# One set of products a batch in place of three, and a new order for the whole program: attention numerators of two batches on 32x32 tiles

## The chip, the cores and the metric

One core of a Trainium2 chip runs the kernel. The metric is the device time of one execution in microseconds (us). Before the change the median of three runs was 218.81 us (217.84 to 220.41).

The engines are named as in the profile: PE (TensorE, matmul), DVE (VectorE), ACT (ScalarE), POOL (GpSimd), and the DMA queues that SP, ACT and POOL feed.

## The reference: what is computed

A polynomial-sketch attention, then a token-mixing block on its output. Cut to what matters:

```python
def phi(x):                                  # r = 8, so 64 features
    a, b = S1 @ x, S2 @ x                    # per batch, head, token
    return outer(a, b)                       # (..., 64)
q_p, k_p = phi(q), phi(k)
kv  = einsum('bhsf,bhsd->bhfd', k_p, v)
num = einsum('bhsf,bhfd->bhsd', q_p, kv)     # what the change rearranges, for batches 2 and 3
den = einsum('bhsf,bhf->bhs', q_p, sum_s k_p) + 1e-6
x = num / den                                # 4 batches, 4 heads of 32, 1088 tokens -> (4, 1088, 128)
theta = x @ w_theta
zr, zi = x * cos(theta), x * sin(theta)
y = w_tok_r @ zr + w_tok_i @ zi              # two 1088 x 1088 mixes per batch
u = x + y
out = u + relu(u @ w_ch)
```

The weights arrive as 64-bit floats; the kernel turns them into 32-bit floats on the chip.

## The kernel before

**Stages.** For each batch: sums over the keys (`sums`, `rest`), key features and their products with v (`kT`, `kf`, `kv`), a small chain that fixes scales (`chain`), query slices (`qT`, `q0`), query features by exact slices (`levels`), the denominator (`den`), the numerator (`num`), theta with its sine and cosine, which gives z (`theta`), then the mix over tokens (`mix`) and the output product (`out`). Tokens are in 9 chunks of 128; three chunks make a group g (0, 1, 2), 384 columns. The rows of `w_tok` come in 17 blocks: each is loaded (L642), converted by two ACT instructions (L643, L645) and two DVE instructions (L647, L649), and only then used by `mix`. Batches 0 and 1 are mixed directly (`mix_row`); 2 and 3 together by seven half-size products (`winograd`: `m1` to `m7`), whose operands POOL and DVE add up (`asum`, `zsub`).

**Order.** Nothing is decided at run time. Every step is an `op` with an engine; the tuple `ORDER` lists all steps in the order in which they are issued, and each engine works its part of that list in order. `STARTS` holds a planned start for each, from which `run` (L248) picks buffers, and from which `issue` (L267) fills planned waits of PE between two marked steps with idle products: `spin` (L427), 384 columns of zeros that nobody reads, five for each planned us (`FILL`). 39 shorter ones (L431) run at the very start.

**Buffers.** Classes of equal buffers (L344): `zs` has 5 of 2176 words (z, the raw weight rows, copies for turning), `g3` 5 of 768, and so on.

**The numerator of batches 2 and 3** (`QUADS`, L1106 to L1123). For each of the three groups, DVE makes the outer products `qp` and turns them in 32x32 blocks into `qt` (class `g3`); `quads` (L1112) then runs 32 products for the group: 2 feature halves f x 4 row blocks j x 4 heads h, each with a 32x32 stationary block and 3 x 32 = 96 moving columns, on the tile of the array at row block j and column block h. f = 0 and f = 1 add up in one PSUM bank for each j. ACT copies the four banks to `xT` (L1121). In the trace an f32 product leaves two matmul records, so that a group has 64.

**The end.** `finish` (L1282) makes the output product, adds it (L1294), turns the result on DVE (L1303) and stores it. For batch 3's first half it starts the stores right there (L1304 to L1307: one on ACT's queue, one on SP's, two on POOL's). The last 160 columns of that half go through `finish_turned` (L1329), where PE turns the columns itself and the two stores write whole rows.

Of the kernel before, what the change touches and what calls it, by code (L numbers as in the profile page):

```python
# [22 lines left out]
P = 128  # L23
# [55 lines left out]
)  # L79
STARTS = (  # L80
# [58 lines left out]
)  # L139
WARM = 0  # L140
FILL = 5.0
LOAD_LEAD = 60.0
RAW_LEAD = 30.0
CHAINS = ((0,), (1,), (2, 3))
# [35 lines left out]
class Layout:  # L180
# [67 lines left out]
    def run(self):  # L248
        slots = {c: [[0.0, None] for _ in range(n)] for c, (n, _) in self.classes.items()}
        for b in self.bufs:  # L250
            b.left = len(b.ops)
# [52 lines left out]
def act(n):  # L304
    return 0.17 + 0.00083 * n
# [1238 lines left out]
```

## Time and profile before

| What | Value |
|---|---|
| Median of three runs | 218.81 us (217.84, 218.81, 220.41) |
| Profiled execution, span from first to last instruction | 215.9 us |
| Median less the span | 2.9 us |
| PE matmul records, of them idle ones (L428) | 2396, 67 |
| Start of the first matmul that is not idle | 4.95 us |
| First token-mix product (`mix0_0`) | 57.16 us |
| End of the last matmul | 212.17 us |
| Granted TensorE clock, mean | 0.995 |

The span is one execution's; the median less the span is what a launch adds around it. How to read the profile's rows: in a timeline row the first number is the start in us, the second the time until the last of the merged instructions ended, `x64` how many there are, and square brackets tell of idle time before. Matmuls overlap, so what a set costs PE is the distance from its start to the start of the next row, not its second number. In a row of groups the numbers after the bar are busy us, mean ns of one, and after the next bar the idle time before them.

### The profile page before, as it was taken

The numbers are of one execution on the slowest core, as the hardware profiler recorded it, in microseconds if no ns is written. First come the engines' busy times: TensorE is split into PE (matmuls) and PEld (weight loads), VectorE is DVE, ScalarE is ACT, GpSimd is POOL, SyncE is SP. The second block draws the span as 40 slices with busy tenths as digits, with TensorE's granted clock in tenths as the row PEclk, the third lists the DMA queues.
The fourth block names the chain that finished last, engine by engine and source line by source line (L and its number), as shares of the span: only waits on it lengthen the run. The fifth ranks groups of instructions, "written<-read, shape, count | busy, mean of one in ns | idle before, by whom it ended". The sixth has DMA issues, their size and how long they took to land.

```text
span 215.9 us, 5832 instructions
## 1 busy us (share of the span) xinstructions
PE 208.9 (97%) x2396; PEld 152.8 (71%) x2396; DVE 174.3 (81%) x343; ACT 114.5 (53%) x256; POOL 59.7 (28%) x105
## 2 busy tenths in 40 slices
PE   7899999999999999999999999999999999999992
PEld 7677798868866666866668666667677776666781
DVE  1799998999999998999999798885994747456263
ACT  4899989999998895798704233363810000000000
POOL 1272740306400000604004100000006489950403
PEclk9999999999999999999999999999999999999998
DMA  6999999995998993192002402424050420010735
GB/s 222 395 418 419 384 365 420 425 315 97 360 285 267 416 432 145 75 308 45 0 0 32 74 3 112 114 109 112 2 88 15 67 39 0 0 23 8 125 55 103
DMA packets 28046, 37.09 MB, mean 172 GB/s; under 512 B 20564, under 2 KB 23044, under 8 KB 25844
## 3 DMA queue, kind: packets, MB, share of 16 engines
q1 hardware_dynamic: 22868, 31.86, 42.4%
q0 software_dynamic: 1552, 3.25, 7.2%
q10 hardware_dynamic: 3600, 1.62, 2.8%
q8 instruction: 19, 0.31, 0.6%
q14 instruction: 7, 0.06, 0.1%
HBM read 29.84 MB, written 4.00 MB: 157 GB/s over the span
## 4 chain that ended last, share of the span: by engine, by line
PE 63%; DMA 18%; ACT 14%; issue 2%; SPq 1%; DVE 1%; POOL 1%; POOLq 0%; ACTq 0%
PE ps L399 61%; DMA zs<-w_tok 13%; DMA big<-k_l 5%; ACT big L645 4%; ACT big L643 3%; ACT lv L1056 1%; PE ps L1131 1%; ACT big L1021 1%; ACT g L1199 1%; ACT g L1202 1%; ACT g L1205 1%; ACT g L1203 1%; POOL out L1299 1%; SPq L671 0%; ACT g L1135 0%
## 5 line engine op out<-in xcount | busy, mean ns | idle before, releaser
L399 PE MATMUL ps<-big,zs 128*128 128x384 f32 (+2 forms) x380 | 110.5, 436 | 0.0
L399 PEld LDWEIGHTS ps<-big,zs 128*128 128x128 f32 x380 | 66.9, 190 | 32.5
L379 POOL TENSOR_TENSOR big<-big,big 128x544 f32<-128x544 f32 x16 | 22.1, 1458 | 48.6 <-DVE big L379 44.6
L399 PE MATMUL ps<-big,big 128*32 128x32 f32 (+2 forms) x352 | 22.8, 234 | 0.0
L643 ACT ACTIVATE big<-zs 128x1088 f32<-128x1088 f32 x17 | 20.9, 1231 | 1.5 <-DMA zs<-w_tok 0.9
L379 DVE CUSTOM_DVE_ANT_0 big<-big,big 128x2176 uint16<-128x2176 uint16 x17 | 21.5, 1275 | 0.0
L645 ACT ACTIVATE big<-zs 128x1088 int32<-128x1088 uint32 (+1 forms) x18 | 21.4, 1194 | 0.3 <-DMA zs<-w_tok 0.3
L1338 ACT COPY big<-ps 80x256 f32<-80x256 f32 x1 | 0.4, 368 | 39.6 <-DMA out<-g 39.6
L399 PEld LDWEIGHTS ps<-big,big 128*32 128x32 f32 (+1 forms) x352 | 15.3, 124 | 6.8 <-issue 0.8
L1276 ACT COPY g<-ps 128x384 f32<-128x384 f32 (+1 forms) x6 | 2.5, 466 | 23.4 <-PE ps L399 23.4
L379 DVE TENSOR_TENSOR big<-big 128x544 f32<-128x544 f32 x8 | 9.5, 1204 | 5.6 <-PE ps L399 5.6
L383 DVE TENSOR_SCALAR big<-big 128x1088 int32<-128x1088 int32 x17 | 12.2, 719 | 0.0
L379 POOL TENSOR_TENSOR mf<-mv,sm 128x32 f32<-128x32 f16 (+1 forms) x3 | 0.8, 262 | 39.1 <-DVE sm L379 39.1
L428 PE MATMUL ps<-idle 128*128 128x112 bf16 (+1 forms) x67 | 10.0, 312 | 1.3 <-POOL idle L430 1.3
L379 DVE TENSOR_TENSOR g<-lv 128x768 f32<-128x768 f32 x12 | 11.1, 950 | 0.1
L399 PEld LDWEIGHTS ps<-w,big 128*128 128x128 f32 (+1 forms) x76 | 9.8, 189 | 1.4
L379 DVE TENSOR_TENSOR big<-big,hf 128x1152 f32<-128x1152 f32 x8 | 10.7, 1351 | 0.0
L399 PE MATMUL ps<-w,big 128*128 128x128 f32 (+1 forms) x76 | 10.5, 278 | 0.0
L399 PE MATMUL ps<-sbk,g 128*128 128x64 f32 x72 | 10.0, 276 | 0.3 <-ACT g L793 0.3
L379 DVE TENSOR_TENSOR zs<-zs,g 128x384 f32<-128x384 f32 (+2 forms) x24 | 9.8, 447 | 0.2
L386 DVE SCALAR_TENSOR_TENSOR big<-ps,even,big 128x384 f32<-128x384 f32 (+1 forms) x10 | 4.8, 493 | 6.3 <-PE ps L399 6.2
L1199 ACT ACTIVATE g<-ps 128x384 f32<-128x384 f32 x12 | 5.9, 504 | 7.3 <-PE ps L399 7.3
(199 smaller groups left out, 379.2 us busy)
## 6 DMA issues: line engine op xcount, KB each, us to landing
zs<-w_tok SPq DMA_DIRECT2D x17, 1088.0 KB, 10.6
big<-k_l SPq DMA_DIRECT2D x5, 576.0 KB, 13.2
big<-v_l SPq DMA_DIRECT2D x4, 576.0 KB, 15.6
big<-q_l SPq DMA_DIRECT2D x3, 576.0 KB, 10.7
big<-hf POOLq DMA_DIRECT2D x3, 576.0 KB, 10.0
far<-zs SPq DMA_DIRECT2D x3, 576.0 KB, 2.8
zs<-far SPq DMA_DIRECT2D x12, 144.0 KB, 4.3
big<-k_l ACTq DMA_DIRECT2D x2, 576.0 KB, 4.4
```

Source lines behind the costliest of these rows:

```text
L379: eng.tensor_tensor(out=o, in0=a, in1=b, op=f)
L383: (eng or V).tensor_scalar(out=o, in0=a, scalar1=s1, scalar2=s2, op0=op0, **kw)
L386: (eng or V).scalar_tensor_tensor(out=o, in0=a, scalar=s, in1=b, op0=op0, op1=op1)
L399: T.matmul(o, lhs, rhs, start=start, stop=stop, skip_group_check=True)
L428: T.matmul(nowhere()[:, :n], idle()[:, 0:P], idle()[:, :n], start=True, stop=True, skip_group_check=True)
L643: op("A", 0.22 + n * 0.0009, lambda: A.activation(dfn(), words_of(raw(), n)[1].bitcast(F32), AF.Prelu, scale=2.0**-112, alpha=-(2.0**32)), ...
L645: op("A", 0.22 + n * 0.0009, lambda: A.activation(stp(), words_of(raw(), n)[0].bitcast(U32), AF.Copy, scale=2.0**-29), [stp], [raw])
L1021: op("A", act(GW) + 0.1, lambda g=g, tr=tr: A.activation(f()[:, g * GW:(g + 1) * GW], tr(), AF.Copy, scale=s()[:, 0:1]), [(f, g)], [tr, (s ...
L1056: op("A", act(480), lambda g=g, lp=lp: A.copy(lv().rearrange("p l (c n) -> p l c n", n=HR)[:, :, g * GC:(g + 1) * GC], lp().rearrange("p c ...
L1131: T.transpose(tr()[:, i * P:(i + 1) * P], qp()[:, i * H + 2 * n:i * H + 2 * n + 2].rearrange("p h i j -> p (h i j)"), ident())
L1199: op("A", act(GW), lambda cs=cs, th=th: A.activation(cs()[:, 0], th(), AF.Copy, bias=ROUND), [(cs, 0)], [th])
L1276: op("A", act(w), lambda: A.copy(u(), yp()[:, :w]), [uT], [yp])
```

## The change

The diff does this:

- **Numerators of batches 2 and 3.** `qt` becomes one buffer a batch for all 9 chunks, in class `zs`, which grows to 2304 words; `g3` goes from 5 buffers to 4. After all three groups are turned, `quads` runs once a batch: the same 32 products with 9 x 32 = 288 columns. Four copies of 288 columns follow in place of twelve of 96.
- **Order.** `ORDER` is replaced as a whole, and with it where every load, conversion, product and store stands on its engine. `STARTS` and `FILL` are gone: buffers come from a list `SLOTS`, and idle products from `GAPS`, 20 in seven places (27 stood in the order before).
- **`finish_turned`.** Two PE steps in place of one, the copy between them is an ACT step, and the result has its own buffer `yb`.
- **`levels`.** In the last chunk only the 64 tokens that exist are the stationary operand.

```diff
+GAPS = {11: 5, 57: 3, 14: 3, 86: 1, 436: 3, 168: 1, 119: 4}
+SLOTS = (
...
     def run(self):
...
         self.order = [self.ops[i] for i in ORDER]
-        for o, at in zip(self.order, STARTS):
...
+        for b, slot in zip([b for b in self.bufs if b.cls is not None], SLOTS):
+            b.slot = slot
...
         for o in self.order:
-            if o.eng == "P":
-                if on:
-                    for _ in range(int((o.start - last - 0.08) * FILL)):
-                        fill()
-                last, on = o.end, on and o is not span[1] or o is span[0]
+            for _ in range(GAPS.get(o.i, 0)):
+                fill()
...
-        "zs": (5, 2176),
+        "zs": (5, 2304),
...
-        "g3": (5, 768),
+        "g3": (4, 768),
...
+                    n = min(P, S - c * P)
+                    x = f()[:, c * P:c * P + n]
+                    mm(o(i)[:n, 2 * HR:], x, mf[b]().rearrange("p t h r -> p (t h r)"), False, i == GC - 1)
...
+        qt = buf("zs", (NC, H, 2, SQ), F32, "qt") if b in QUADS else None
...
-                qt = buf("g3", (GC, H, 2, SQ), F32, "qt")
-                xq = [buf("ps", (GC, SQ), F32, "xq") for _ in range(NQ)]
...
+                vop(CH * R * R, lambda g=g, qp=qp: V.transpose(
+                    out=qt()[:, g * GC:(g + 1) * GC].rearrange("p c h f t -> p (c h f t)"),
+                    in_=qp().rearrange("p n i j -> p (n i j)")), [(qt, g)], [qp])
                 continue
...
+        if b in QUADS:
+            at("num", b)
+            xq = [buf("ps", (NC, SQ), F32, "xq") for _ in range(NQ)]
+
+            def quads():
+                for f in range(2):
+                    for j in range(NQ):
+                        for h in range(H):
+                            u = slice(j * SQ, (j + 1) * SQ)
+                            mm(xq[j]()[h * D:(h + 1) * D], bd()[u, f, h], qt()[u, :, h, f], f == 0, f == 1)
+
+            op("P", QUAD, quads, xq, [bd, qt], hold=[xt])
...
-            for c, uc in enumerate(parts):
-                T.transpose(pu()[:n, c * DM:(c + 1) * DM], uc, ident())
-            A.copy(y(), pu()[:n, 0:2 * DM])
-            for c, uc in enumerate(parts):
-                mm(po()[:n, c * DM:(c + 1) * DM], uc, w2()[:, 1], True, True)
...
+        op("P", 0.2, turned, [pu], keys, hold=[yb])
+        op("A", act(2 * DM), lambda: A.copy(y(), pu()[:n, 0:2 * DM]), [yb], [pu])
+        op("P", 0.35, products, [po], keys + [w2])
```

At the very end of the program the new order also swaps neighbours: the last product of PE is now that of batch 3's first 384 columns (a `finish` with four stores of turned columns), where it was `finish_turned`.

More of the change, by code (lines that the diff above doesn't have):

```diff
@@ L34 @@
 ORDER = (
[44 rows of a table removed]
-)
-STARTS = (
[58 rows of a table removed]
[43 rows of a table added]
+)
+GAPS = {11: 5, 57: 3, 14: 3, 86: 1, 436: 3, 168: 1, 119: 4}
+SLOTS = (
[11 rows of a table added]
 )
 WARM = 0
-FILL = 5.0
 LOAD_LEAD = 60.0
@@ L157 @@
 UDMA = (True, True, False, False)
-TILE16, TILE32, TILE64, QUAD = 0.045, 0.12, 0.15, 0.65
+TILE16, TILE32, TILE64, QUAD = 0.045, 0.12, 0.15, 1.25
 ADD_FLY = 9.0
@@ L248, in run, with issue @@
     def run(self):
-        slots = {c: [[0.0, None] for _ in range(n)] for c, (n, _) in self.classes.items()}
-        for b in self.bufs:
-            b.left = len(b.ops)
         self.order = [self.ops[i] for i in ORDER]
-        for o, at in zip(self.order, STARTS):
-            o.start = at / 100.0
-            o.end = o.start + o.dur + o.fly
-            for b in o.bufs:
-                if b.slot is None and b.cls is not None:
-                    free = [(s[0], i) for i, s in enumerate(slots[b.cls]) if s[1] is None]
-                    b.slot = min(free)[1]
-                    slots[b.cls][b.slot][1] = b
-            for b in o.bufs:
-                b.left -= 1
-                b.end = max(b.end, o.end)
-                if not b.left and b.slot is not None:
-                    slots[b.cls][b.slot] = [b.end, None]
-    def issue(self, pools, fill, span):
-        last, on = 0.0, False
-        for o in self.order:
-            if o.eng == "P":
-                if on:
-                    for _ in range(int((o.start - last - 0.08) * FILL)):
-                        fill()
-                last, on = o.end, on and o is not span[1] or o is span[0]
+        for b, slot in zip([b for b in self.bufs if b.cls is not None], SLOTS):
+            b.slot = slot
+    def issue(self, pools, fill):
+        for o in self.order:
+            for _ in range(GAPS.get(o.i, 0)):
+                fill()
             for b in o.bufs:
@@ L430 @@
     op("G", 0.3, lambda: G.memset(idle(), 0.0), [idle], [], due=-20.0)
-    first = op("P", 3.2, lambda: [spin(112) for _ in range(39)], [nowhere], [idle], due=-10.0)
+    op("P", 3.2, lambda: [spin(112) for _ in range(39)], [nowhere], [idle], due=-10.0)
     op("V", 1.25, constants, [hm, bdm, halfpi, ones], [])
@@ L1050, in whole @@
                 for i in range(GC):
-                    x = f()[:, (g * GC + i) * P:(g * GC + i + 1) * P]
-                    mm(o(i)[:, 2 * HR:], x, mf[b]().rearrange("p t h r -> p (t h r)"), False, i == GC - 1)
+                    c = g * GC + i
+                    n = min(P, S - c * P)
+                    x = f()[:, c * P:c * P + n]
+                    mm(o(i)[:n, 2 * HR:], x, mf[b]().rearrange("p t h r -> p (t h r)"), False, i == GC - 1)
             op("P", 0.4, exact, [lp], [h, mv[b]], hold=[lv])
@@ L1106, in outputs_x @@
             if b in QUADS:
-                qt = buf("g3", (GC, H, 2, SQ), F32, "qt")
-                xq = [buf("ps", (GC, SQ), F32, "xq") for _ in range(NQ)]
-                vop(CH * R * R, lambda qt=qt, qp=qp: V.transpose(out=qt().rearrange("p c h f t -> p (c h f t)"),
-                                                                 in_=qp().rearrange("p n i j -> p (n i j)")), [qt], [qp])
-                def quads(qt=qt, xq=xq):
-                    for f in range(2):
-                        for j in range(NQ):
-                            for h in range(H):
-                                u = slice(j * SQ, (j + 1) * SQ)
-                                mm(xq[j]()[h * D:(h + 1) * D], bd()[u, f, h], qt()[u, :, h, f], f == 0, f == 1)
-                op("P", QUAD, quads, xq, [bd, qt], hold=[xt])
-                for j in range(NQ):
-                    op("A", act(GC * SQ), lambda g=g, j=j, xq=xq: A.copy(
-                        xt().rearrange("p (c j t) -> p c j t", j=NQ, t=SQ)[:, g * GC:(g + 1) * GC, j], xq[j]()),
-                       cells(xt, g * GW, (g + 1) * GW), [xq[j]])
+                vop(CH * R * R, lambda g=g, qp=qp: V.transpose(
+                    out=qt()[:, g * GC:(g + 1) * GC].rearrange("p c h f t -> p (c h f t)"),
+                    in_=qp().rearrange("p n i j -> p (n i j)")), [(qt, g)], [qp])
                 continue
@@ L1145, in outputs_x @@
                cells(xt, g * GW, (g + 1) * GW), [xp])
+        if b in QUADS:
[8 more added lines that the diff above has]
+            op("P", QUAD, quads, xq, [bd, qt], hold=[xt])
+            for j in range(NQ):
+                op("A", act(NC * SQ), lambda j=j: A.copy(
+                    xt().rearrange("p (c j t) -> p c j t", j=NQ, t=SQ)[:, :, j], xq[j]()), [(xt, ("q", j)) if j < NQ - 1 else xt], [xq[j]])
         src = xt
@@ L1331, in finish_turned, with turned @@
         n = w // 2
-        y = lambda: xT[b]()[:n, 0:2 * DM]
-        def products():
-            parts = [u()[:, c * n:(c + 1) * n] for c in range(2)]
-            for c, uc in enumerate(parts):
-                T.transpose(pu()[:n, c * DM:(c + 1) * DM], uc, ident())
-            A.copy(y(), pu()[:n, 0:2 * DM])
-            for c, uc in enumerate(parts):
-                mm(po()[:n, c * DM:(c + 1) * DM], uc, w2()[:, 1], True, True)
-        op("P", w * 4 / 2400 + 0.01, products, [po, pu], keys + [w2])
-        vop(w, lambda: stt(y(), po()[:n, 0:2 * DM], 0.0, y(), ALU.max, ALU.add), keys, [po])
-        vop(w, lambda: None, [], keys)
+        yb = buf("g1", (2 * DM,), F32, "yb")
+        y = lambda: yb()[:n]
+        def turned():
+            for c in range(2):
+                T.transpose(pu()[:n, c * DM:(c + 1) * DM], u()[:, c * n:(c + 1) * n], ident())
+        def products():
+            for c in range(2):
+                mm(po()[:n, c * DM:(c + 1) * DM], u()[:, c * n:(c + 1) * n], w2()[:, 1], True, True)
+        op("P", 0.2, turned, [pu], keys, hold=[yb])
+        op("A", act(2 * DM), lambda: A.copy(y(), pu()[:n, 0:2 * DM]), [yb], [pu])
+        op("P", 0.35, products, [po], keys + [w2])
+        vop(2 * DM, lambda: stt(y(), po()[:n, 0:2 * DM], 0.0, y(), ALU.max, ALU.add), [yb], [po])
         def store(E, c):
             E.dma_start(out[b, t0 + c * n:t0 + (c + 1) * n, :], y()[:, c * DM:(c + 1) * DM])
-        op("S", w * P * 2 / 100e3, lambda: store(SY, 0), [], keys, due, lk=2)
-        op("A", 0.92, lambda: store(A, 1), [], keys, due, fly=2.1)
+        op("S", w * P * 2 / 100e3, lambda: store(SY, 0), [], [yb], due, lk=2)
+        op("A", 0.92, lambda: store(A, 1), [], [yb], due, fly=2.1)
     def winograd(t):
@@ L1469 @@
         if not bs[0]:
-            last = op("P", 0.1, spin, [nowhere], [kvb[WARM]] if WARM < B else [idle])
+            op("P", 0.1, spin, [nowhere], [kvb[WARM]] if WARM < B else [idle])
     for b in range(B):
@@ L1499 @@
     with tc.manual_schedule():
-        L.issue(pools, spin, (first, last))
+        L.issue(pools, spin)
 def kernel(q, k, v, S1, S2, moe_w_theta, moe_w_tok_r, moe_w_tok_i, moe_w_ch):
```

156 rows, old and new, of tables (ORDER, SLOTS, STARTS) are left out of this document.

## The prediction

> **What bounds the kernel now.** I read the page's busy times and slices first, then busy time by stages.
>
> ```profile
> PE 208.9 (97%) x2396; PEld 152.8 (71%) x2396; DVE 174.3 (81%) x343; ACT 114.5 (53%) x256; POOL 59.7 (28%) x105
> ...
> DVE  1799998999999998999999798885994747456263
> ...
> PEclk9999999999999999999999999999999999999998
> ```
>
> ```profile
> 0.00:57.20 57.20, 54.23 (x1097) 45.63 (x1097) 49.34 (x124) 51.00 (x125) 21.60 (x62) 1.00 0.94 348
> 57.20:98.00 40.80, 40.75 (x443) 28.21 (x440) 39.47 (x67) 35.61 (x62) 3.44 (x8) 1.00 0.80 276
> 98.00:156.00 58.00, 58.00 (x618) 39.39 (x617) 51.59 (x88) 25.89 (x68) 5.40 (x8) 1.00 0.20 53
> 156.00:212.20 56.20, 55.96 (x246) 39.56 (x244) 33.52 (x67) 1.96 (x5) 28.50 (x26) 1.00 0.27 45
> ```
>
> In the stage rows the third number is PE's busy time, the fifth DVE's, then ACT's and POOL's. From 98 us PE never stops: what is taken from it there comes off the end. From 57 to 98 us PE and DVE are both full. Before 57 us PE's 54 us include idle products, and DVE and ACT (49 and 51 us of 57) set the pace. In the third, DVE reaches each row's conversion just before PE uses it.
>
> Then PE's timeline and the groups by shape, for prices:
>
> ```profile
> 20.50 0.20 PE L399 MATMUL ps<-hf 128*32 128x32 bf16 x4
> 20.63 0.55 PE L1018 MATMUL ps<-ident,big 128*128 128x128 f32 x3
> ...
> 119.09 0.96 PE L399 MATMUL ps<-g,g 32*32 32x96 f32 x64
> 119.98 3.39 PE L399 MATMUL ps<-big,zs 128*128 128x384 f32 x10
> ...
> 163.18 0.81 PE L399 MATMUL ps<-big,zs 128*128 128x384 f32 x2
> 163.83 0.81 PE L399 MATMUL ps<-big,big 128*128 128x384 f32 x2
> ```
>
> ```profile
> L428 PE MATMUL ps<-idle 128*128 128x384 bf16 x28 | 6.2, 327 | 0.0
> ...
> L1121 ACT COPY big<-ps 128x96 f32<-128x96 f32 x24 | 4.3, 252 | 10.1 <-PE ps L399 10.0
> ```
>
> A set of 64 records costs 119.98 - 119.09 = 0.89 us; six sets, 5.34 us. A 384-column record costs 0.645 / 2 = 0.323 us, 0.84 ns a column. The first pair shows a change of tile shape: four records take 0.13 us where in a run they take 0.03. Over the trace, going from 128x128 to 128x32 tiles costs 0.093 us and back 0.119, so a pair 0.21; into 32x32 tiles 0.093, and back 0.164.
>
> **The change part by part**, against the profiled execution's 215.9 us; the launch's 2.9 us (median 218.81 less span) is put back at the end.
>
> *Numerators.* Each of the 16 tiles works four records one after another: f twice, two records a product. At 96 columns that streams 4 x 0.081 = 0.32 us of the 0.89; 0.57 is issue, weights and the change of shape. At 288 columns streaming is 4 x 0.242 = 0.97. If it hides the rest, a set costs 1.0; if the two add up, 1.54; if all grows with the columns, 2.67. I take 1.35, between the first two and nearer the sum, since in the trace the second 16 records wait until the first are through. Two sets: 2.7, so 2.64 less. Four entries into 32x32 go (4 x 0.093 = 0.37), and the mix product behind each set takes 0.75 where 0.645 is usual (4 x 0.10 = 0.4). Sum -3.4, from -4.1 to -0.8. All lies between 119 and 136 us, where PE is full.
>
> [...]
>
> *Copies.* ACT does 8 of 288 columns for 24 of 96: between 252 ns and the 492 of a 384-column copy, some 0.41, so 3.3 us for 6.0. A batch's theta now waits for four copies in a row, 1.6 us; the new order puts 2.6 us of mix products between the set and the first theta. Cost nothing; 0 to 1 us if that cover is gone. `qt` is ready later, but DVE's turns stand some 4 us ahead of the sets.
>
> *The first stage.* I added up PE's work in both orders, each step at its median in the trace. Before, 47.3 us of PE's work precede the first mix product, at 57.16 us: a lag of 9.9 (1.34 until the first product, 27 x 0.163 = 4.4 idle products, the rest waits and changes of shape). In the new order 48.5 us precede it, 1.2 more. Against it stand 24 more changes of shape there (73 for 49), mostly 12 pairs between 128x128 and 128x32: 12 x 0.21 = 2.5 us. For it, 7 idle products fewer, 1.1 us. If all of that lies on PE's path, the first mix product starts at 1.34 + 48.5 + 2.5 + 20 x 0.163 + 4.2 (the rest as before) = 59.8: 2.6 later with 1.2 more done, +1.4 us. If DVE sets the start: before, at its tightest places, PE's summed work was 3.2 us less than what DVE had to have done (row 9's conversion); in the new order at most 1.3. PE can then run 1.9 us earlier, -1.9. I take a lag of 9.0, start at 57.5: (57.5 - 57.16) - 1.2 = -0.9, nearer to DVE's end, since the waits that the extra changes fall into are DVE's.
>
> *The end.* Before, PE ends at 212.17; `finish_turned` then needs DVE 0.42, two stores issued at once, landed at 214.76, and 1.13 of closing: 3.7 us.
>
> ```profile
> 210.30 0.57 DVE L1303 STREAM_TRANSPOSE g<-big 128x384 f32<-128x384 f32 x1
> ...
> 212.28 0.42 DVE L386 SCALAR_TENSOR_TENSOR big<-ps,big 80x256 f32<-80x256 f32 x1 [0.40 <-PE ps L399]
> ...
> 211.17 1.81 POOL L1299 DMA_DIRECT2D out<-g  x3 [0.50 <-DVE g L1303]
> ```
>
> Now last, the 384-column `finish` needs 0.56 and 0.57 (overlapping, 1.08) on DVE, then two stores one after the other on POOL's queue: from the turn's end (210.87) to the second's landing (214.0) 3.13 us. With the closing 5.3: +1.6 us, from 0 to +2.
>
> *The rest at nothing.* The split of `finish_turned` (a 0.27 product stands in its wait), the shorter weights in `levels` (the 96 columns that stream are the same), one `g3` buffer fewer, the instruction fetches (19 of 16 KB before, each about 1 us, with no unexplained stop at them). If the cover fails, 0 to 0.5 us each.
>
> Sum: 215.9 - 3.4 - 0.9 + 1.6 = 213.2; with 2.9, **216.1 us**.
>
> **Rivals.**
>
> *The products grow with their columns* (2.67 a set): the numerators give 0.8 alone, 215.9 - 0.8 - 0.9 + 1.6 = 215.8, so 218.7: no change. Against: only 0.32 of 0.89 us streams. Chance 0.10.
>
> *The new changes of shape are all on the path*: +1.4 in place of -0.9, 215.5, so 218.4: no change. For it: each is 0.09 to 0.12 us in the trace wherever PE is fed; against: they replace idle products. Chance 0.20. [...]
>
> *Late rows, the slow side.* Weight rows are loaded into class `zs`, which has 5 buffers as before, but now `qt` holds one too, from DVE's turns of batch 2 until its set. The new order converts the last rows late: by DVE's sums, rows 13, 14 and 16 are done 99.0, 105.4 and 113.2 us into its work; with DVE's 7 us of idle time at 106, 112 and 120. PE's products with them come at 111, 115.5 and 123. The slack is 3 to 5 us. A load of a row took 10.6 us (median, issue to landing). If one load waits for a buffer for longer than the slack, PE, which works in order, stops: one load's 10.6 less 5 is 5.6 us, 218.8, so 221.7. It decides once a row comes 5 us later than these sums. Against: in this stretch the DMA share is down to 0.20. Chance 0.17.
>
> **How the numbers follow.** The forecast has 0.53; its own range, 213.5 to 217.8, comes from -4.1 and -1.9 with +1.6, and from 1.35 becoming 1.54, the lag staying as before and the end at +2. A measurement of this kernel tells about 1% (2.2 us; its three runs spread over 2.6) from no change, so faster is under 216.6, slower over 221.0. Of the forecast some 0.06 lies above 216.6, and of the second rival 0.03 below: faster 0.50, within 1% 0.33, slower 0.17. The range: 212.5 leaves out better luck at the end (0.05), 221.5 the worse half of the late rows (0.09).
>
> **What would show it.** Two rows of 64 records with 288 columns, 1.0 to 1.55 us from their start to the next row's. The first mix product at 56.5 to 59. No idle time over 1 us before a mix product between 95 and 125 us (the late rows). PE full from there, ending near 207.9, and a tail of about 5.3 us with POOL's stores last. A granted clock of 1.00 throughout: a stretch at 0.5, as in the first 5.3 us, would make all wrong, and so would a first mix product after 60 us.

## The result and the profile after

The changed kernel took 234.94 us (median of 4 runs, 233.87 to 239.57) where the kernel before took 218.49 in the same comparison: a ratio of 1.073, interval 1.066 to 1.080. It is slower by 16.5 us, where 216.1 was predicted. The profiled execution has a span of 232.1 us; the prediction's sum was 213.2, so 18.9 us have to be found.

The page's busy time and slices, of the changed kernel:

```profile
PE 216.1 (93%) x2133; PEld 157.2 (68%) x2133; DVE 179.0 (77%) x343; ACT 114.9 (50%) x240; POOL 66.2 (29%) x105
...
PE   7999999698799999999999999999999989979990
...
PEclk9975699999999999999999999999999999999997
```

PE has fewer instructions and is "busy" 7 us longer, and the clock row has a hole between 12 and 29 us. Busy time by stretches puts numbers on it (PE's busy time is the third number of a row; the granted clock, the DMA share and GB/s are the last three). All rows are of the changed kernel:

```profile
7.22:10.63 3.41, 3.20 (x49) 1.83 (x47) 3.21 (x11) 3.38 (x9) 1.76 (x2) 1.00 1.02 405
10.63:14.04 3.41, 3.01 (x114) 2.81 (x114) 3.10 (x9) 2.51 (x11) 1.70 (x4) 1.00 1.01 410
14.04:27.70 13.66, 13.66 (x150) 12.40 (x150) 8.32 (x18) 7.45 (x25) 7.59 (x24) 0.50 1.03 381
...
0.00:71.00 71.00, 63.92 (x1216) 54.21 (x1217) 49.86 (x125) 49.85 (x128) 25.27 (x62) 0.90 0.86 292
...
172.00:225.90 53.90, 51.15 (x221) 35.41 (x219) 34.33 (x63) 0.37 (x1) 24.75 (x19) 1.00 0.15 25
```

From 14.04 to 27.70 PE ran at half clock (0.50). The first mix product starts at 70.99 (57.5 predicted, 57.16 before):

```profile
70.99 2.32 PE L332 MATMUL ps<-big,zs 128*128 128x384 f32 x7
```

And in the last row of the stretches PE misses 2.75 us in a stage where it was to be full. PE's waits in the changed kernel, with what ended each, in us, times, and the longest:

```profile
PE ps L332 <- issue: 3.3, 3, 2.3
PE ps L951 <- issue: 1.8, 1, 1.8
...
PE ps L332 <- POOL big L312: 1.3, 1, 1.3
PE ps L332 <- DVE g L319: 0.9, 1, 0.9
PE ps L332 <- DVE big L312: 0.5, 1, 0.5
```

"issue" is idle time that no semaphore explains: 5.1 us in four stops, all before 60 us. The trace says where they are. Counted by start, PE's records at which it resumed (products, weight loads and the semaphore instructions between them, without the drain that opens the program) are the 961st, 1473rd, 1729th and 1985th; each is 193 more than a multiple of 256. One packet of 16 KB in the queue "instruction" lands a little ahead of each. The same pieces, before and after (us):

| piece begins at record | before: fetch landed | before: PE is there | after: fetch landed | after: PE resumes |
|---|---|---|---|---|
| 961 | 26.85 | 29.45 | 30.75 | 32.04 (stopped 0.31) |
| 1473 | 39.11 | 41.81 | 44.36 | 45.90 (stopped 1.81) |
| 1729 | 45.19 | 50.50 | 50.92 | 52.36 (stopped 0.62) |
| 1985 | 50.59 | 55.09 | 58.25 | 59.58 (stopped 2.34) |

PE resumes 1.3 to 1.5 us after its piece of program has landed. Before, each piece had landed 2.6 to 5.3 us early; with those 1.3 to 1.5 us taken off, little more than a microsecond was to spare at the first, and no wait showed it.

The sets themselves, in PE's timeline of the changed kernel, and then the end of it:

```profile
141.34 1.60 PE L332 MATMUL ps<-zs,g 32*32 32x288 f32 x64
142.87 2.85 PE L332 MATMUL ps<-big,zs 128*128 128x384 f32 x8
...
226.47 0.58 DVE L1240 STREAM_TRANSPOSE g<-big 128x384 f32<-128x384 f32 x1
...
227.34 1.86 POOL L1236 DMA_DIRECT2D out<-g  x3 [0.96 <-DVE g L1240]
```

A set costs 142.87 - 141.34 = 1.53 us (1.35 predicted). At the end POOL issues three stores one after another, not two; the tail from PE's end to the span's end is 6.25 us (5.3 predicted).

So the 18.9 us are: 13.5 until the first mix product (of it 5.1 stops and at most half of 13.65, 6.8, of clock), 4.4 between it and PE's end (of it 2.7 in three late waits and 0.4 in the two sets; some 1.3 us stay unaccounted for), and 1.0 in the tail. The theory to test: the old order with its idle products kept clock and program ahead, the new one loses both. The rivals: the order itself is late by DVE's and ACT's chain, the stops are waits for data, the merged products cost something later, or POOL causes the late waits.

### The profile page after: what moved, and what is told of

The parts are those of the page before. It is cut to its first block, busy times and chain, and to the rows that moved or that the text cites. A ratio compares the mean times of both kernels' runs of the same rounds, so it can differ in the third digit from the quotient of the medians.

```text
span 232.1 us, 5283 instructions
## 1 busy us (share of the span) xinstructions
PE 216.1 (93%) x2133; PEld 157.2 (68%) x2133; DVE 179.0 (77%) x343; ACT 114.9 (50%) x240; POOL 66.2 (29%) x105
## 4 chain that ended last, share of the span: by engine, by line
PE 83%; DVE 6%; POOL 4%; issue 3%; DMA 2%; ACT 0%; POOLq 0%; SPq 0%; DVEq 0%; ACTq 0%
PE ps L332 75%; DVE big L312 2%; POOL big L312 2%; PE ps L723 2%; DMA st<-s 2%; PE ps L1053 2%; PE ps L951 2%; DVE zs L312 1%; PE ps L361 1%; POOL sbk L312 1%; PE ps L1126 1%; POOL out L1236 1%; DVE g L1240 0%; DVE hf L316 0%; POOLq L1479 0%
## 5 line engine op out<-in xcount | busy, mean ns | idle before, releaser
L332 PE MATMUL ps<-big,zs 128*128 128x384 f32 (+2 forms) x380 | 108.6, 436 | 2.2 <-POOL big L312 1.3
L312 POOL TENSOR_TENSOR big<-big,big 128x544 f32<-128x544 f32 x16 | 23.4, 1488 | 13.3 <-DVE big L312 13.1
L326 POOL DMA_DIRECT2D g<-big x6 | 5.4, 949 | 47.7 <-ACT g L1213 36.5
L1236 POOL DMA_DIRECT2D out<-g x8 | 5.1, 642 | 27.0 <-DVE g L319 17.0
L332 PE MATMUL ps<-sbk,g 128*128 128x64 f32 x72 | 11.7, 312 | 0.3 <-POOL sbk L312 0.3
L312 POOL TENSOR_TENSOR mf<-mv,sm 128x32 f32<-128x32 f16 (+1 forms) x3 | 1.9, 634 | 32.6 <-DVE sm L312 32.6
L332 PEld LDWEIGHTS <-hf 128*32 128x32 bf16 (+1 forms) x252 | 7.7, 96 | 4.9 <-issue 3.0
L332 PEld LDWEIGHTS ps<-sbk,g 128*128 128x128 f32 x72 | 10.5, 223 | 0.6 <-POOL sbk L312 0.4
L332 PE MATMUL ps<-mf,big 128*128 128x96 f32 (+1 forms) x72 | 10.6, 282 | 0.0
## 6 DMA issues: line engine op xcount, KB each, us to landing
big<-k_l SPq DMA_DIRECT2D x5, 576.0 KB, 12.7
```

What stands on the lines that cost most here:

```text
L312: eng.tensor_tensor(out=o, in0=a, in1=b, op=f)
L326: op("G", 0.9, lambda: G.dma_start(dst(), src(), accum_op=ALU.add), w, r, fly=fly)
L332: T.matmul(o, lhs, rhs, start=start, stop=stop, skip_group_check=True)
L1236: E.dma_start(out[b, s0:s0 + n, f * SQ:(f + 1) * SQ].rearrange("(c j) i -> j c i", j=SQ), ot()[f * SQ:(f + 1) * SQ, :n].rearrange("j (c i) ...
```

## The experiments

**Merged products in the old order.** The kernel before, with one set a batch; a place in ORDER holds batch 2's set, another batch 3's.

```diff
-    qt = buf("g3", (GC, H, 2, SQ), F32, "qt")
+    if g == 0:
+        qt = buf("zs", (NC, H, 2, SQ), F32, "qt")
...
+    if g != {2: 1, 3: 2}[b]:
+        op("P", 0.0, lambda: None, [], [])
+        continue
```

> The kernel before in its own order, with only the merged numerators (one set of 64 records of 288 columns for each of batches 2 and 3, at the place of batch 2's second set and of batch 3's last; theta of batch 3's first group moved behind it). If the prediction's term for the products is right and the loss of the changed kernel comes from its new order alone: two rows of 1.53 us for six of 0.89, so 2.3 us less, with four entries into 32x32 fewer 2.3 to 3.4 less, 215.0 to 216.5 us, and a granted clock of 1.00 from 6 us on. If the merged sets themselves cost something later (the four copies in a row before theta, banks of PSUM held longer): 217.5 to 220, with PE's idle time before theta's products of batch 2.

219.53 us, ratio 1.003 (0.999 to 1.008): no gain. PE's timeline of this kernel shows why:

```profile
129.97 1.35 PE L399 MATMUL ps<-big,zs 128*128 128x384 f32 x4
134.08 2.09 PE L399 MATMUL ps<-zs,g 32*32 32x288 f32 x64 [2.76 <-DVE zs L1110]
```

Two sets fewer ahead of it, PE came to batch 3's set 2.76 us before DVE had turned the last third. It then paid twice, as busy time by the clock's stretches shows:

```profile
131.30:134.72 3.42, 0.66 (x34) 0.48 (x34) 3.38 (x5) 0.05 (x1) 0.00 (x0) 1.00 0.43 172
134.72:138.13 3.41, 3.41 (x51) 1.60 (x34) 2.56 (x4) 1.71 (x5) 0.00 (x0) 0.50 0.44 122
```

The 3.41 us behind the idle stretch ran at half clock, and the set itself took 2.02 us. Neither reading of the expectation was whole: the products are cheaper, but the place was wrong.

**The set moved later.** Same kernel, batch 3's set behind four more of batch 1's mix products.

```diff
-    ... 766, 860, 767, 770, 858, 775, 633, 771, 712, 772, 526, 773, 716, 774, 782, 634, ...
+    ... 766, 860, 767, 858, 775, 633, 712, 634, 635, 613, 716, 770, 771, 526, 772, 773, 660, ...
```

> As the merged numerators in the old order, with batch 3's set behind four more of batch 1's mix products (its copies and theta's products behind them). There PE waited 2.76 us for DVE's turn of the last third, and the clock's next 3.4 us were granted at 0.5. Wait theory (the merged sets' gain of 2.3 us is there, and the wait and the half clock behind it ate it): no wait ahead of the set, no stretch at 0.5 near it, the set 1.53 us, 214.5 to 216.5 us against 218.4 before (ratio 0.983 to 0.991). Rival (wide sets themselves bring the half clock, or theta and balance behind them become late): a stretch at 0.5 again, or a new wait behind 140 us, 217.5 to 219.5.

216.44 us, ratio 0.993 (0.991 to 0.995), with no stretch at 0.5 and the set at 1.52 us. The wait theory holds. Of the 2.76 us, 0.17 is left ahead of the set, and a longer wait has come further on:

```profile
145.14 2.47 PE L399 MATMUL ps<-big,zs 128*128 128x384 f32 x8 [1.11 <-DVE g L386]
```

**And that wait filled:** DVE's relu step of theta (operation 784) moved ahead of the sums 719, 726 and 600.

> As the merged numerators with batch 3's set moved behind four mix products, and DVE's relu step of theta of batch 3's first group moved ahead of six sums of batches 1 and 2. There PE waited 1.11 us at 144 for the bank that this step frees. If that wait is all: PE's end 1.1 us earlier, 215.0 to 215.8 us (ratio 0.985 to 0.989). If the sums that now stand behind it are waited for: 216 to 217 us, with a new wait between 142 and 150.

215.82 us, ratio 0.989 (0.985 to 0.994). This version beats both kernels: 2.1 us less than before. Its profiled execution is its slowest, 218.98 us: the clock was at 0.5 for 3.41 us from 80.48, behind a wait of 1.24 us for ACT.

**Idle products put back into the new order** (17 of them; the expectation says 19).

```diff
-GAPS = {11: 5, 57: 3, 14: 3, 86: 1, 436: 3, 168: 1, 119: 4}
+GAPS = {11: 5, 57: 3, 14: 3, 64: 2, 98: 1, 65: 1, 67: 1, 140: 1, 110: 1, 134: 2, 73: 2, 79: 1, 104: 1, 245: 2,
+        126: 1, 197: 1, 86: 1, 436: 3, 168: 1, 119: 4}
```

> The changed kernel with 19 more idle products of 384 columns, put in PE's waits between 9.5 and 22 us, where the new order has none. Clock theory (PE's sparse work there lets the clock fall to 0.5 for 13.65 us, and the lag this leaves makes PE run through its instructions faster than they are fetched): granted clock 1.00 throughout from 8 us, first mix product 4 to 10 us earlier than 70.99, 224 to 230 us. Order theory (the new order is late by DVE's and ACT's chain, whatever the clock): clock 1.00, but the first mix product still at 69 to 73 and 233 to 237 us. If the idle products do not hold the clock: a stretch at 0.5 of over 8 us remains, 234 us or more.

The first expectation was nearly met, and in the profiled execution alone (230.23 us, where 224 to 230 was expected): the first mix product came at 67.34, 3.65 us earlier (4 to 10 expected), and the clock was 1.00 until 31:

```profile
PEclk9999979999999999999999999999999999999997
```

The median of all runs was 235.24 (230.23 to 240.23), no better than the changed kernel. In the profiled run a stop of 2.17 us at record 961 came first, and a stretch of 3.41 us at 0.5 behind it. The idle products held the clock until then; this stop, at which the program was not there, they could not fill.

**52 records fewer at the start**, at equal time.

```diff
-    op("P", 3.2, lambda: [spin(112) for _ in range(39)], [nowhere], [idle], due=-10.0)
+    op("P", 3.2, lambda: [spin(336) for _ in range(13)], [nowhere], [idle], due=-10.0)
```

> The changed kernel with 13 idle products of 336 columns at the start for 39 of 112: the same time of PE, 52 records fewer in its program. Page theory (PE stops where a 16 KB piece of its program, 256 records, is not there yet): the unexplained stops stay at the same counts of records from the start (961, 1473, 1729, 1985 of products and weight loads), so 52 records further in the work, before other instructions than now. Wait theory (each stop is a wait for data or for an engine that the trace does not name): the stops stay before the same instructions (line 951's transposes at 45.9 us among them). The time is no test: 233 to 236 us by either.

The stops are at records 449 (3.15 us), 1217 (1.47), 1729 (1.57) and 1985 (0.47, which the profile puts down to DVE): other pieces, but each 193 above a multiple of 256, while the work under these counts has moved by 52 records. The stop before line 951 is gone. Every stop of over 0.4 us before the first mix product that was put down to "issue", in all eight profiles of the new order, was at such a count. So the stops come from pieces of the program, not from data; which piece is late changes from kernel to kernel.

**Weight rows half loaded** (their second halves are left out), so that 9.5 MB less go through the queues.

```diff
-    op("S", n * 1024 / 380e3, lambda: SY.dma_start(raw(), src), [raw], [], lead=RAW_LEAD)
+    op("S", n * 1024 / 380e3, lambda: SY.dma_start(raw()[:, :h], src[:, :h]), [raw], [], lead=RAW_LEAD)
...
```

> The changed kernel with only the first half of each weight row's words loaded (its conversion reads them twice): 9.5 MB less through the DMA queues, the same instructions on PE, DVE and ACT; the weights' second halves are left out. If the stops come from pieces of the program that wait behind the bulk loads: from PE's entry into one piece to the start of the next piece's fetch under 3 us (1.7 to 4.9 in the changed kernel), unexplained stops under 1.5 us in all for 5.1, fewer stretches at 0.5, first mix product at 60 to 64 (59.5, and half of the time at 0.5), 220 to 227 us. If they come from PE's pace or from a fetch that always takes this long: stops of 3 to 6 us in all, first mix product at 66 to 71, 230 us or more.

One stop is left, of 1.0 us (5.1 in the changed kernel). From entering a piece to the start of the next one's fetch it took 0.2 to 3.6 us, where the changed kernel needed up to 4.9. So the row loads are part of what the fetches wait behind; they are not all of it, since in the next run, with the same loads, one fetch still began 4.5 us after its piece ahead was entered. The time missed its expectation, 230.41 (226.72 to 233.61) for 220 to 227: the clock still fell at 13.9 us, without any stop ahead of it, and the first mix product was at 66.47 (60 to 64 expected).

**Both together**, half the row loads and the 17 idle products.

> The changed kernel with both: the weight rows' words half loaded (second halves left out) and the 17 more idle products in PE's waits between 9.5 and 22 us. If the account of the first stage is whole (the new order by itself reaches the first mix product at 59.5, each idle product adds up to 0.16, each stop its length, each us at 0.5 half a us): clock 1.00 from 8 us in most runs, stops under 1.5 us, first mix product at 60.5 to 63, 220 to 224 us. If the clock falls for a third cause, or the order is later than 59.5 by itself: a stretch at 0.5 though no stop is before it, or the first mix product at 65 or more with neither, 226 us or more.

225.57 us (225.12 to 225.93) in all four runs; first mix product at 63.03 (60.5 to 63 expected), one stop of 0.9. The clock row of its page:

```profile
PEclk9999999999999999999999999999999999999996
```

The account of the first stage held; the total, 220 to 224, was set too low, because behind the first mix product this kernel is as the changed one: 154.9 us to PE's end in both. Clock and stops (all but 0.9 us) were 9.4 us of the 16.5, net of up to 2.8 us that the added idle products cost. The rest can be read from the spans, 224.2 us here and 215.9 before: 5.9 us more until the first mix product (2.8 of them the idle products, 0.9 the stop), nothing between it and PE's end (154.9 for 155.0), and 2.5 in the tail (6.26 for 3.73). So what the merged sets gained behind the first mix product is spent there again, mostly in the late waits.

**The mirror: 13 idle products out of the old order**, those from 12.7 to 16.4 us.

```diff
-    fill()
+    nf += 1
+    if not 7 <= nf <= 19:
+        fill()
```

> The kernel before without 13 of its 27 idle products, those from 12.7 to 16.4 us (none is left from 8.4 to 22 us, as in the changed kernel). Theory of clock, lag and pages: one to four stretches of 3.4 us at 0.5 between 12 and 28 us in most runs, PE behind by 2 to 7 us, then running through its program faster than it is fetched: unexplained stops at records of the count 193 mod 256; 221 to 232 us, and a wider spread of its runs. Rival (the old order needs no idle products; the clock of the changed kernel falls for another cause): clock 1.00, 217 to 219 us.

220.42 us, ratio 1.010 (1.006 to 1.013). The clock fell as expected: 0.5 for 6.83 us from 19.4, behind a wait of 1.88 us for ACT; the mean clock was 0.975 to 0.990 in all four runs. The clock row of its page:

```profile
PEclk9997699999999999999999999999999999999998
```

The stops did not come, and the loss was 2.3 us, not 3 to 14. So a fall of the clock does not by itself run PE out of program in the old order.

**12 changes of tile shape more in the old order.**

```diff
+    if o.i in (203, 197, 257, 205, 120, 251, 443, 440, 335, 341, 339, 193):
+        thin()   # matmul, 128 rows x 32 columns of weights, 32 columns
```

> The kernel before with 12 small products of a 128x32 tile, each between two products of 128x128 tiles, from 15 to 41 us: 12 pairs of changes of tile shape more, as the new order has. If changes of shape are on PE's path there (12 times 0.21 + 0.02): first mix product at 59.5 to 60.0 (57.16 before), 220.7 to 221.5 us. If they fall into waits for DVE (the prediction's choice): first mix product at 57.0 to 57.6, 218 to 219 us. 24 more records also move the pieces of the program; a stop at one of them would show by its count.

220.76 us, ratio 1.012 (1.010 to 1.014). PE came to its first mix product at 59.0, 1.85 later for 2.8 us of such work, so two thirds are on the path. There it stopped:

```profile
60.74 1.21 PE L401 MATMUL ps<-big,zs 128*128 128x384 f32 x3 [1.73 <-DVE big L385]
```

The profile names DVE, but DVE's step had ended at 59.01. The record is the 2241st, 193 + 8 x 256, and its piece landed at 59.4: a piece of the program again. The 24 records more have pushed this boundary behind a run of small products: PE took 2.9 us from record 1985 to here.

**Three sets of 96 columns in place of one of 288**, in the changed kernel.

> The changed kernel with three sets of 96 columns one after another where it has one of 288 (the same buffers, copies and order). If what a set costs beside streaming its columns is paid once for each set: 2.5 to 2.7 us for the three, 1.0 to 1.15 more in each batch, PE's end 2.0 to 2.3 us later, about 237 us. If the cost goes by columns alone: 1.5 us as now, 235 us. If PE has slack behind the sets: the rows as in the first case, the end as now.

```profile
137.81 2.42 PE L332 MATMUL ps<-zs,g 32*32 32x96 f32 x192
140.16 2.85 PE L332 MATMUL ps<-big,zs 128*128 128x384 f32 x8
```

2.35 us for three, 0.82 more a batch (1.0 to 1.15 expected), and from the first mix product to PE's end 156.5 us for 154.9: all of it on the path. Its 232.0 us are below the changed kernel's, since its clock was at 0.5 for 6.8 us, not 13.7: in this order a single time says little of a change of 2 us.

**Eight of POOL's sums on DVE** (`APOOL = ("4",)`), and POOL's odd store (operation 994) ahead of batch 3's last.

> The changed kernel with the eight sums of product 7 on DVE where they were on POOL, and POOL's store of batch 2's last half row put ahead of batch 3's last two. If the late stops come from POOL's 13 sums in a row (1.49 us each where 0.73 on DVE): the stop of 1.26 us before product 7's second half is gone and the one before batch 3's last row shorter; from product 5's first to the end of PE 50.0 to 50.3 us where it was 51.2. If from DVE: the stops stay. The tail behind PE's end: 5.6 us for 6.25 if it was the third store that ended last, the same if not.

The stop of 1.26 us is gone, and one of 2.15 us for DVE came earlier; product 5's first to PE's end took 52.3 us (51.2). That idea failed. The tail became 5.65 us: the third store had ended last.

**POOL's sums for products 3 and 7 left out.**

> The changed kernel without POOL's 13 to 16 sums for products 3 and 7 (left out: those products read their operands unsummed). If the late stops (0.48 before product 6, 0.95 before batch 3's last rows, 1.26 in product 7) come from POOL, which is waited for and slows DVE's sums beside it (1.04 to 1.25 us each where 0.70 alone): all three gone, DVE's sums 0.70 throughout, from product 5's first to the end of PE 48.0 to 48.6 us for 51.2. If the order sets PE behind DVE's sums too closely by itself: the first two stay and only the third goes, 49.6 to 50.0 us.

All three late waits are gone: 47.8 us, 3.4 less. The same three sums of DVE in its timeline, first in the changed kernel and then here:

```profile
185.33 3.13 DVE L312 TENSOR_TENSOR big<-big 128x544 f32<-128x544 f32 x3 [0.52 <-PE ps L332]
```

```profile
186.04 1.99 DVE L312 TENSOR_TENSOR big<-big 128x544 f32<-128x544 f32 x3
```

So DVE's sums take longer beside POOL's, 1.04 us each for 0.66. In the kernel before it was as bad (DVE's and POOL's timelines), and PE's rows show no wait there, presumably since products that need nothing from DVE stood there:

```profile
177.13 4.59 DVE L379 TENSOR_TENSOR big<-big 128x544 f32<-128x544 f32 x1 [2.70 <-PE ps L399]
...
175.66 5.47 POOL L379 TENSOR_TENSOR big<-big,big 128x544 f32<-128x544 f32 x4
```

A sum of this shape takes 0.72 us elsewhere in that trace; this one took 4.59 and ended 0.6 us after POOL's four (175.66 to 181.13) were through, as if it had not got in between them. What holds it up there is not shown.

## Why the prediction was wrong

**The step that failed is the first stage**, "a lag of 9.0, start at 57.5", with the fetches costed at nothing ("no unexplained stop at them", 0 to 0.5 us if their cover fails; they cost 5.1) and the clock taken as 1.00 (it cost up to 6.8). The first mix product of seven profiles, with the stops' length, half of the time at 0.5 and 0.163 for each added idle product taken off:

| kernel | first mix product | stops | us at 0.5 | what is left |
|---|---|---|---|---|
| changed | 70.99 | 5.1 | 13.65 | 59.1 |
| idle products back | 67.34 | 3.5 | 3.41 | 59.3 |
| 52 records fewer | 69.45 | 6.7 | 6.83 | 59.4 |
| three sets | 67.46 | 4.6 | 6.83 | 59.5 |
| sums on DVE | 69.44 | 3.5 | 13.65 | 59.1 |
| rows half loaded | 66.47 | 1.0 | 13.65 | 58.6 |
| half rows, idle products | 63.03 | 0.9 | 0 | 59.3 |

(Without POOL's sums the clock was at 0.5 for 27.3 us; with half of that taken off, 57.3 would be left, and why it differs is open.) The new order by itself is thus at some 59 us, as an estimate: a lag of 10.6 behind its 48.5 us of work, where the prediction chose 9.0 and its rival with all changes of shape on the path had 11.3 (59.8). That lies nearer to the rival, as does the run with 12 changes of shape more (two thirds on the path). The choice went to DVE's end because the waits into which the extra changes fall were taken to be DVE's; the idle products that filled waits were counted as a cost saved (7 x 0.163), not as what held the clock.

**Point by point.** *Numerators:* the mechanism was right, a set was mis-sized: 1.53 for 1.35, the end at which streaming and the rest add up (1.54). That is 0.36 of -3.4; the version with the products in the old order gained 2.1 (interval 1.4 to 3.2). *Copies:* no wait at theta, as said. *Tail:* 6.25 for 5.3; an old store was queued on POOL behind the two that were counted. *From the first mix product on:* "PE full from there" failed by 2.7 us of waits that POOL's sums make; the prediction looked at PE's lag against the rows and never at how long a sum of DVE lasts beside POOL. *Late rows:* did not happen; there is no wait over 1 us between 95 and 125 us. *What would make it wrong* named both signs that came, a stretch at 0.5 and a first mix product after 60, but neither had a price or a chance, so the range ended at 221.5. *Sums:* the terms named for the lower end of the forecast's own range (-4.1, -1.9, +1.6) add up to 214.4, not 213.5. The 2.9 us put back at the end mix two executions: run by run the time is 1.7 to 2.0 us above the span (217.84 for 215.9, 233.87 for 232.1). The reason given for 1.35 was misread too: in the set of before the first 32 records start 7 ns apart, and it is the 33rd that waits. None of the three bears on the miss.

**Why the fetches failed it.** "No unexplained stop" was read as free. The trace of before had the margins in it: for each of the first six fetches, the fetch began 2.3 to 3.5 us after PE had entered the piece ahead of it and took 1 us; with the 1.3 us from there until PE resumes, PE would have stopped there, as an estimate, if it had run 256 records in less than 4.6 to 5.8 us. The old order took 5.7 to 8.7 for these six. This is no fixed limit: its seventh piece ahead took 4.59 without a stop, because the fetch had begun 0.8 us before PE entered it, and in the new order fetches began up to 4.9 us after, and PE stopped behind four pieces that had 4.9 to 6.5 us of work. Why they began later there is not settled. The traces show the size of a piece in the counts (193 above multiples of 256) and in the packets of 16 KB; coming to one that was late cost up to 3.15 us (record 449, with 52 records fewer).

**What stays open:** why the clock fell at 14 us. No share of busy time parts the stretches of 3.41 us ahead of a fall from the others. Six falls came behind a stretch in which PE was busy for 19 to 55%, with a wait or stop of 1.5 to 3.2 us in it, and one (the last version of the old order, at 80.48) behind 64%. Yet in the run with 12 changes of shape more, 49% was followed by none, and neither were many of 57 to 90%. Ahead of 14.04 PE was busy for 88%, in 114 small products, by a row shown above. In the traces the fall goes with how the time is cut into such stretches: in the four profiles in which the clock fell at 13 to 14 us, the stretch ahead began at 9.7 to 10.6 us and PE was busy for 79 to 88% of it; with three sets and with 52 records fewer, the same early order had a stretch that began at 11.1, PE was busy for 92% of it, and the clock stayed at 1.00 until a stop further on. The added idle products are what kept it in the last combination (99% busy in the stretch from 11.84, mean clock 0.991 to 0.997 in its four runs; with half the row loads alone it fell). What decides it was not shown.

## What to carry to other kernels

Idle products in PE's waits are not waste: without 13 of them the old order had its clock at 0.5 for 6.83 us and lost 2.3 us. Before an order takes them out, look at how busy PE stays in each stretch of 3.41 us: here it was 79 to 88% ahead of the falls at 13 to 14 us, and 92 or 99% where the clock held, though no share parts the two throughout. Count PE's records in 256s against the fetches of its program: here, at a DMA share of 0.80 (27.7 to 71 us of the changed kernel), four pieces of 256 records with 4.9 to 6.5 us of work were through before the next had landed, and a stop could have a halved clock behind it (2.17 us, then 3.41 us at 0.5). When products get cheaper, move what feeds them too: the same edit gave nothing with its set in the old place and 2.1 us with four products moved ahead of it.

## What the runs showed of the hardware

All stretches at 0.5 before PE's end, behind the start, are multiples of 3.41 us (1 to 5 of them), and their phase differs from trace to trace (the clock first goes to 1.00 at 4.26 to 7.22 us: at 5.57 in the kernel before, where the prediction had 5.3, and at 7.22 in the changed one, whose next changes are at 14.04 and 27.70). In the kernel before, records of 128 f32 columns start some 213 ns apart until then and 109 ns apart behind it. Runs of one kernel differ by up to 10 us, 230.23 at a mean clock of 0.986 and 240.23 at 0.932; that the phase is the reason is likely, but only one run of each kernel has a trace. One fall came behind a stretch with a wait of 1.88 us, a little over half of 3.41 (ahead of 19.4 us, in the old order without 13 idle products).
